# Two-stage attention and a maxout layer on one core: another form of the pooling sums, and the main order without its list of departures

## The chip, the cores and the metric

The kernel runs on one core of a Trainium2 chip. TensorE (PE in the profile) multiplies matrices; a multiplication is a weight load (PEld) and a matmul, and its sums go to PSUM, eight banks of 128 partitions by 512 fp32 numbers. VectorE (DVE), ScalarE (ACT) and GpSimd (POOL) work on tiles; SyncE (SP) and POOL issue transfers. Each engine takes its own instructions in the order in which the program gives them, and waits for others by semaphores. The metric is the time of one execution in microseconds (us) on the device, the median of several; less is better.

## The reference

The input is x of 4 batches by 12,544 tokens by 128 channels, 32 inducing points of 128 channels, and the three weights of a maxout layer with 1,024 hidden units. All is fp32.

```python
def mab(q, kv):
    s = scale * (q @ kv.transpose(0, 2, 1))
    s = s - s.max(-1, keepdims=True)
    a = np.exp(s)
    a /= a.sum(-1, keepdims=True) + 1e-09
    return a @ kv
h = mab(I, x)          # pooling: 32 rows per batch, each a mean of the batch's tokens
y = mab(x, h)          # each token: a mean of its batch's 32 rows of h
g = np.maximum(y @ w1, y @ w2)
out = g @ w_out
```

So each batch must first be pooled over all its tokens to h, and only then can its tokens go through the second attention and the layer.

## The kernel before

**The main part.** Each token's y is a mean of 32 rows of h, weighted by e = exp(scale x h). So the layer is taken on h first: `hwd` is h (w2 - w1) and `m1` belongs to h w1 w_out; a block of 16 chunks of 128 tokens lies in four quarters of 32 partitions each. Per block PE makes e by a *stage* (four matmuls, column mode: four tiles of 32 columns side by side), then *phases* (`phase`, L969 in the profile, row mode: four tiles of 32 rows side by side), whose results are passed through a relu by ACT (L985) or DVE (L988), then *finals* (`final_one`, L792, the full array), 3,136 of them, 128 x 128 each, which multiply the relus by w_out and sum over the hidden units. `dens` (L622) sums e to denominators, `evict_group` (L819) divides and stores through SP.

**The pooling of the next batch** runs beside it, batches 1 to 3. The tokens of a batch are 98 chunks: six units of 16 and a rest of two. Its steps:

- `load_x` (POOL) brings x in seven parts as fp16; a small copy to `pace` holds these loads back until a given sum is there.
- `transpose_x_dma` (L171) has SP transpose x by transfers, 14 half parts; the first unit's scores need the first three of them.
- `pool_scores` (L309, column mode) makes the scores of a unit; ACT makes exp of them, E, and their sums into a column of `es` (L320). `pool_turn` (L346) has SP transpose E to `eT`.
- `pool_accum` (L357, column mode) sums E x over a unit's chunks in one bank of PSUM; DVE adds the bank to `hacc` in SBUF (L382, L385). After the last unit the rest's two chunks are added (L370), with their sums of E in a 129th column.
- `small_rep` (L401) sums the sums of E over the four groups of partitions by an fp32 matmul with `repd`; DVE takes the reciprocal and scales `hacc` (L404, L406). `small_h` (L430) sums h over the groups and transposes it by another fp32 matmul. `small_hwd` (L464) and `small_m1` (L484) follow.

**What sets the order.** The order of each engine's instructions is written when the program is made, by a planner in Python: a class `Clock` (`ck`) adds up what each step is charged, `bank` takes the PSUM bank that comes free first, and a loop chooses the next step for PE. Side steps have due times, counted in finished chunks (`at`), and are ready when the clock says that their inputs are (`ready`). Column steps (scores, accumulations, stages) are taken by `column_work` when PE is in column mode anyway, when two are waiting, or when one is late. A change of the array's mode is charged about 0.1 us. In the loop a list, `DEV`, gives 84 numbered steps at which the choice departs from the rule: 1 puts a phase off, 2 takes it up to 0.2 us earlier, 3 leaves column work out, 4 takes it at once.

The rule itself, and how `DEV` alters it:

```python
now = tp <= ck.pe + early or tp <= tf and tf > ck.pe
if how == 1 and tf < INF:
    now = False
if how == 2 and tp <= ck.pe + 0.2:
    now = True
```

Of the kernel before, what the change touches and what calls it, by code (L numbers as in the profile page):

```python
# [9 lines left out]
F16 = mybir.dt.float16  # L10
F32 = mybir.dt.float32
# [5 lines left out]
INF = 1e9  # L17
# [85 lines left out]
def kernel(  # L103
# [93 lines left out]
    with tc.manual_schedule(engines={ET.PE, ET.DVE, ET.Activation, ET.Pool, ET.SP}):  # L197
# [103 lines left out]

        def pool_scores(b, u):
            if u == 0:
                st[b]["es"] = smp.tile([128, NU + 1], F32, name=f"es_{b}", tag="esu")
                nc.gpsimd.memset(st[b]["es"], 0.0)
            bi, ps = bank([128, 512])
            ck.wait(ck.bank[bi], "p1")
            for g in range(4):
                nc.tensor.matmul(  # L309
                    out=ps[32 * g : 32 * (g + 1), :],  # L310
                    lhsT=inducingT,
                    rhs=xT_tiles[b % 2][:, U * u + 4 * g : U * u + 4 * (g + 1), :],
                    start=True,
                    stop=True,
                    tile_position=(0, 32 * g),
                    skip_group_check=True,
                )
            end = ck.run(0.226, "col")
            eu = etp.tile([128, 512], F16, name=f"eu_{b}_{u}", tag="eu", bufs=NEU)
            nc.scalar.activation(  # L320
                out=eu, in_=ps, func=AF.Exp, scale=scale, accum_out=st[b]["es"][:, u : u + 1]
            )
            ck.bank[bi] = ck.on_act(end, 0.65)
            st[b]["eu", u] = eu, ck.bank[bi]
# [22 lines left out]
            st[b]["eT", u] = eT, ck.pe  # L347

        def pool_accum(b, u):
            bi, ps = bank([128, 512])  # L350
            ck.wait(ck.bank[bi], "p1")
            eT = st[b]["eT", u][0]
            st[b]["sum", u] = True
            last = u == NU - 1
            for j in range(4):
                for g in range(4):
                    nc.tensor.matmul(  # L357
                        out=ps[32 * g : 32 * (g + 1), 0:128],
                        lhsT=eT[:, j, 32 * g : 32 * (g + 1)],
                        rhs=xn_of(b, U * u + 4 * g + j),  # L360
                        start=(j == 0),
                        stop=(j == 3 and not (last and g < REST)),
                        tile_position=(0, 32 * g),
                        skip_group_check=True,
                    )
            if last:
                et = st[b]["et"][0]
                for g in range(REST):
                    for rhs, lo, n in ((xn_of(b, U * NU + g), 0, 128), (ones16[:, 0:1], 128, 1)):
                        nc.tensor.matmul(  # L370
                            out=ps[32 * g : 32 * (g + 1), lo : lo + n],
                            lhsT=et[:, g, :],
                            rhs=rhs,
                            start=False,
                            stop=True,
                            tile_position=(0, 32 * g),
                            skip_group_check=True,
                        )
            end = ck.run(0.26, "col")
            if u == 0:  # L380
                st[b]["hacc"] = smp.tile([128, C], F32, name=f"hacc_{b}", tag="hacc")
                nc.vector.tensor_copy(out=st[b]["hacc"], in_=ps[:, 0:128])  # L382
            else:
                acc = st[b]["hacc"]
                nc.vector.tensor_add(out=acc, in0=ps[:, 0:128], in1=acc)  # L385
            ck.bank[bi] = ck.on_dve(end, 0.2)
            if last:
                es = st[b]["es"]
                nc.vector.tensor_copy(out=es[0 : 32 * REST, NU : NU + 1], in_=ps[0 : 32 * REST, 128:129])
                esr = smp.tile([128, 1], F32, name=f"esr_{b}", tag="esr")  # L390
                nc.vector.reduce_sum(out=esr, in_=es, axis=AX.X)  # L391
                st[b]["esr"] = esr
                ck.bank[bi] = st[b]["esrr"] = ck.on_dve(end, 0.2)
                if b + 1 < B:
                    for i in range(7):
                        load_x(b + 1, i, esr if i == 0 else None)

        def small_rep(b):
            bi, ps = bank([128, 512])
            ck.wait(ck.bank[bi], "p1")  # L400
            nc.tensor.matmul(out=ps[:, 0:1], lhsT=repd, rhs=st[b]["esr"], start=True, stop=True)  # L401
            end = ck.run(0.11)
            rec = smp.tile([128, 1], F32, name=f"rec_{b}", tag="rec")
            nc.vector.reciprocal(out=rec, in_=ps[:, 0:1])  # L404
            acc = st[b]["hacc"]
            nc.vector.tensor_scalar(out=acc, in0=acc, scalar1=rec, scalar2=None, op0=ALU.mult)  # L406
            ck.bank[bi] = st[b]["haccr"] = ck.on_dve(end, 0.4)

        def small_h(b):
            hT4 = smp.tile([C, 4, M], F16, name=f"hT4_{b}", tag="hT4")  # L410
            if b == 0:
# [13 lines left out]
                ready = ck.on_act(st[0]["end"], 0.2)  # L425
                st[b]["hT4"] = hT4.rearrange("c q m -> c (q m)")
                return es, ready
            bi, ps = bank([128, 512])
            ck.wait(ck.bank[bi], "p1")
            nc.tensor.matmul(out=ps[:, 0:128], lhsT=st[b]["hacc"], rhs=repd, start=True, stop=True)  # L430
            end = ck.run(0.25)
            nc.vector.tensor_copy(out=hT4.rearrange("c q m -> c (q m)"), in_=ps[:, 0:128])
            ck.bank[bi] = st[b]["hT4r"] = ck.on_dve(end, 0.2)
            st[b]["hT4"] = hT4.rearrange("c q m -> c (q m)")
# [434 lines left out]
        def want_linear():  # L869
# [9 lines left out]
            return g  # L879

        LINEAR_AHEAD = 18


        DEV = {
            0: 1, 27: 1, 32: 1, 35: 2, 52: 1, 87: 2, 157: 3, 168: 1, 169: 4, 181: 2, 244: 2, 247: 1, 397: 4,
            443: 3, 469: 4, 476: 1, 495: 1, 518: 1, 527: 4, 539: 3, 558: 3, 636: 2, 690: 1, 751: 1, 758: 4,
            764: 3, 765: 1, 773: 1, 778: 1, 835: 1, 858: 1, 866: 1, 867: 1, 869: 1, 972: 1, 992: 4, 1011: 2,
            1013: 3, 1014: 4, 1025: 2, 1029: 1, 1052: 1, 1083: 2, 1113: 1, 1125: 1, 1141: 2, 1179: 1, 1195:
            1, 1215: 4, 1216: 1, 1271: 1, 1296: 2, 1301: 1, 1305: 1, 1324: 1, 1357: 1, 1358: 1, 1387: 4,
            1407: 4, 1428: 1, 1460: 4, 1462: 1, 1488: 4, 1491: 1, 1575: 1, 1579: 1, 1580: 1, 1585: 4, 1601:  # L890
            3, 1625: 2, 1658: 3, 1723: 1, 1736: 3, 1739: 1, 1764: 1, 1777: 1, 1796: 4, 1801: 3, 1812: 1,
            1843: 1, 1966: 3, 1981: 1, 1997: 1, 2021: 1
        }
        LIMIT = -16

        def plan_phase(linear=True):
# [106 lines left out]
        for b in range(1, B):  # L1003
            base = DONE0[b - 1]
            t_first, t_step = (6, 2.2) if b == 1 else (-6, 3.4)
            for u in range(NU):
                if b == 1:
                    s, turn, acc = 25 + 5 * u, 45 + 1.5 * u, 55 + 2 * u
                else:
                    s = turn = 13 + 8.2 * u  # L1010
                    acc = s + 12
                at(base + int(s), pool_scores, b, u)
                at(base + int(turn), pool_turn, b, u)
                at(base + int(acc), pool_accum, b, u)
            s, end = int(s), base + int(acc)
            at(base + s + 2, pool_rest, b)
            at(end, small_rep, b)
            at(end, small_h, b)
            at(end, small_hwd, b)
            at(end, small_m1, b)  # L1020
            for j in range(14):
                at(base + int(t_first + t_step * j), transpose_x_dma, b, j)
# [45 lines left out]
                pending.remove(job)  # L1068
                f(*a)

        def column_work(banks, soon=False):

            if sorted(ck.bank)[banks - 1] > ck.pe + 0.12:
                return False
# [3 lines left out]
                return True  # L1078
            jobs = [job for job in pending if job[0] in COL and ready(*job)]
            late = jobs and (chunks_done[0] >= due[jobs[0]] + 8 or jobs[0][1][1] == NU - 1)  # L1080
            if jobs and (soon or ck.mode == "col" or len(jobs) > 1 or late):
                pending.remove(jobs[0])
                f, a = jobs[0]
                f(*a)
# [14 lines left out]
                "hT4" in st[qu.b] and "hwd" in st[qu.b] for qu in blocks[k0].quarters if qu  # L1099
            )  # L1100


        phase(plan_phase(False))
        weights_3()
        phase(plan_phase(False))
# [1 line left out]
        state["stage"] = 2  # L1107
        weights_1b()
        START = ck.pe
        step = -1  # L1110
        while state["g"] < len(groups) or held:
            step += 1
            how = DEV.get(step, 0)
            side_work()
            if held and ck.mode == "full":
                linear_last(0.0)
            if ck.mode != "full" and how != 3 and column_work(1):
                continue
            if min(ck.bank) <= ck.pe + 0.1 and want_stage(1):
                stage(blocks[state["stage"]])  # L1120
# [7 lines left out]
                fr = sorted(ck.bank)[len(jobs) - 1]  # L1128
                tp = max([fr - 0.095] + [(a.blk.staged if kind == "L" else a.staged) for kind, q, a, u in jobs])
            early = 0.2 if ck.mode == "col" else 0.0  # L1130
            now = tp <= ck.pe + early or tp <= tf and tf > ck.pe
            if how == 1 and tf < INF:
                now = False
            if how == 2 and tp <= ck.pe + 0.2:
                now = True
            if tp < INF and lag() <= 128 + LIMIT and now:
                if how != 3 and column_work(len(jobs) + 1, how == 4):
                    continue
                phase(jobs)
            elif tf < INF:  # L1140
# [8 lines left out]
            else:  # L1149
                raise AssertionError(("stuck", state, ptr, chunks_done, jobs, pending[:3]))  # L1150
        assert not pending and not jobs_at

# [28 lines left out]
```

## Time and profile before

| what | value |
|---|---|
| time, median of 3 runs | 329.54 us (329.04 to 329.61) |
| profiled execution, its own time | 329.54 us |
| its span, first to last instruction | 327.6 us |
| PE busy | 321.6 us, 98% |
| DVE busy | 284.8 us, 87% |
| ACT busy | 281.0 us, 86% |
| finals (L792), steps | 3,136 |
| the add to `hacc` (L385), each of 15 | 0.288 us |

A group of the profile is one line and engine with its output and inputs; `xN` is how many instructions it has, then their busy time and the mean of one, then the idle time of the engine ahead of them and what ended it. The lengths of PE's instructions overlap, since matmuls are pipelined: what a step costs is read from the start of one matmul to the start of the next, not from its length. The chain of waits follows the work that ended last back to the start. In the timeline a row is a run of equal instructions: its start, its length, the engine, the line and the tiles. The transfers are listed by queue (q1 is that of SP's transfers, q0 that of POOL's): packets, megabytes, and the share of 16 engines' time in the stretch asked for; and by issue: how many, and how long from issue to landing.

### The profile page before, as it was taken

The numbers are of one execution on the slowest core, as the hardware profiler recorded it, in microseconds if no ns is written. First come the engines' busy times: TensorE is split into PE (matmuls) and PEld (weight loads), VectorE is DVE, ScalarE is ACT, GpSimd is POOL, SyncE is SP. The second block draws the span as 40 slices with busy tenths as digits, with TensorE's granted clock in tenths as the row PEclk, the third lists the DMA queues.
The fourth block names the chain that finished last, engine by engine and source line by source line (L and its number), as shares of the span: only waits on it lengthen the run. The fifth ranks groups of instructions, "written<-read, shape, count | busy, mean of one in ns | idle before, by whom it ended". The sixth has DMA issues, their size and how long they took to land.

```text
span 327.6 us, 12592 instructions
## 1 busy us (share of the span) xinstructions
PE 321.6 (98%) x5401; PEld 243.8 (74%) x5401; DVE 284.8 (87%) x532; ACT 281.0 (86%) x562; POOL 25.8 (8%) x54
## 2 busy tenths in 40 slices
PE   7999999999999999999999999999999999999996
PEld 3886777777777777777777777777777777778785
DVE  2359998999989999998989989989999989989873
ACT  3679899998789998988988999989969999899961
POOL 7451030000310000000040000000000000000000
PEclk9999999999999999999999999999999999999999
DMA  7999999964299998953579999992422212222233
GB/s 205 207 207 211 288 247 205 236 150 139 57 228 244 228 232 204 197 131 109 121 131 246 217 257 207 182 187 98 132 98 79 101 66 100 98 98 99 83 114 113
DMA packets 70823, 53.65 MB, mean 164 GB/s; under 512 B 52176, under 2 KB 55408, under 8 KB 70768
## 3 DMA queue, kind: packets, MB, share of 16 engines
q1 hardware_dynamic: 64656, 38.63, 47.8%
q0 software_dynamic: 6112, 14.22, 22.2%
q8 instruction: 42, 0.69, 0.9%
q14 instruction: 13, 0.11, 0.1%
HBM read 28.33 MB, written 25.69 MB: 165 GB/s over the span
## 4 chain that ended last, share of the span: by engine, by line
PE 94%; DVE 2%; ACT 1%; DMA 1%; issue 1%; DVEq 0%; ACTq 0%
PE ps L792 60%; PE ps L969 22%; PE ps L582 3%; PE ps L232 2%; PE ps L357 1%; PE ps L309 1%; DMA xf<-in_x_dram 1%; PE ps L248 1%; ACT relu L985 1%; DVE relu L988 1%; PE ps L280 1%; PE ps L622 1%; PE ps L749 1%; PE ps L271 1%; PE ps L640 0%
## 5 line engine op out<-in xcount | busy, mean ns | idle before, releaser
L985 ACT ACTIVATE relu<-ps 128x512 f16<-128x512 f32 x463 | 244.8, 603 | 28.9 <-PE ps L969 20.6
L988 DVE TENSOR_SCALAR relu<-ps 128x512 f16<-128x512 f32 x321 | 205.6, 681 | 18.2 <-PE ps L969 17.3
L792 PE MATMUL ps<-woutp,relu 128*128 128x128 f16 x3136 | 218.1, 220 | 0.1
L792 PEld LDWEIGHTS <-relu 128*128 128x128 f16 x3136 | 177.2, 98 | 40.4 <-issue 30.1
L969 PE MATMUL ps<-e,hwd 32*128 32x512 f16 (+2 forms) x880 | 88.6, 360 | 0.0
L819 DVE TENSOR_TENSOR o<-ps,rp 128x512 f32<-128x512 f32 (+3 forms) x108 | 68.5, 635 | 6.0 <-PE ps L792 3.7
L969 PEld LDWEIGHTS <-hwd 32*128 32x128 f16 x880 | 24.7, 91 | 21.0 <-issue 0.8
L969 PE MATMUL ps<-m,e 32*128 32x128 f16 x381 | 38.7, 217 | 0.0
L969 PEld LDWEIGHTS <-e 32*128 32x128 f16 x381 | 21.4, 92 | 2.6
L165 POOL DMA_DIRECT2D xn<-in_x_dram x31 | 16.9, 555 | 8.2 <-DMA xn<-in_x_dram 4.3
L236 DVE COPY xT<-ps 128x512 f16<-128x512 f16 (+3 forms) x11 | 5.5, 504 | 8.1 <-PE ps L232 8.0
L594 ACT ACTIVATE e<-ps 128x512 f16<-128x512 f32 (+2 forms) x21 | 11.6, 570 | 0.0
L320 ACT ACTIVATE eu<-ps 128x512 f16<-128x512 f32 x18 | 10.8, 616 | 0.0
L582 PE MATMUL ps<-xT,hT 128*32 128x512 f16 (+3 forms) x114 | 10.2, 366 | 0.0
L164 POOL COPY pace<-esr 128x1 f32<-128x1 f32 x2 | 0.4, 184 | 116.2 <-DVE esr L391 116.2
L239 ACT COPY xT<-ps 128x768 f16<-128x768 f16 (+3 forms) x11 | 6.1, 557 | 3.0 <-PE ps L232 2.8
L232 PE MATMUL ps<-identity,xn 128*128 128x128 f16 x98 | 7.7, 223 | 0.2
L232 PEld LDWEIGHTS <-xn 128*128 128x128 f16 x98 | 5.9, 100 | 1.5 <-DVE xn L644 1.0
L582 PEld LDWEIGHTS <-hT 128*32 128x32 f16 x114 | 2.9, 93 | 5.3 <-issue 4.2
L257 ACT ACTIVATE et<-ps 128x448 f16<-128x448 f32 (+4 forms) x11 | 4.5, 413 | 2.6 <-PE ps L248 2.6
L632 DVE RECIPROCAL rp<-ps 128x16 f32<-128x16 f32 (+2 forms) x28 | 6.7, 239 | 0.0
L622 PE MATMUL ps<-ones_q,e 128*128 128x4 f16 x102 | 6.5, 165 | 0.0
(96 smaller groups left out, 117.0 us busy)
## 6 DMA issues: line engine op xcount, KB each, us to landing
out_dram<-o SPq DMA_DIRECT2D x90, 256.0 KB, 2.5
xn<-in_x_dram POOLq DMA_DIRECT2D x24, 448.0 KB, 11.9
out_dram<-o SPq DMA_DIRECT2D x10, 128.0 KB, 3.7
xn<-in_moe_w_dram POOLq DMA_DIRECT2D x4, 256.0 KB, 14.1
xn<-in_x_dram POOLq DMA_DIRECT2D x4, 224.0 KB, 10.2
xT<-xn SPq DMA_TRANSPOSE x42, 3.9
xf<-in_x_dram SPq DMA_DIRECT2D x1, 512.0 KB, 3.8
xf<-in_x_dram SPq DMA_DIRECT2D x1, 384.0 KB, 4.3
```

Source lines behind the costliest of these rows:

```text
L165: nc.gpsimd.dma_start(out=xn_at[b, i][:, 0:n, :], in_=xr[b, :, k0 : k0 + n, :])
L232: nc.tensor.transpose(ps[:, j, :], xn[:, g + j, :], identity16)
L320: nc.scalar.activation(out=eu, in_=ps, func=AF.Exp, scale=scale, accum_out=st[b]["es"][:, u : u + 1])
L582: nc.tensor.matmul(out=ps[32 * q : 32 * (q + 1), 128 * t : 128 * (t + n)], lhsT=hq, rhs=xT[:, c : c + n, :], start=True, stop=True, tile_p ...
L594: nc.scalar.activation(out=blk.e2[:, 0 : 128 * wd], in_=ps[:, 0 : 128 * wd], func=AF.Exp, scale=st[0]["rs"] if blk.b == 0 else scale,)
L622: nc.tensor.matmul(out=ps[:, 4 * t : 4 * t + 4], lhsT=blk.e2[:, 128 * t : 128 * (t + 1)], rhs=ones_q, start=True, stop=True,)
L632: nc.vector.reciprocal(out=blk.rp[:, 0:wd, :].rearrange("p t q -> p (t q)"), in_=ps[:, 0 : 4 * wd])
L792: nc.tensor.matmul(out=g.ps[:, 128 * c : 128 * (c + 1)], lhsT=g.blk.relu[q][:, 128 * (jb * w4 + t) : 128 * (jb * w4 + t + 1)], rhs=woutp[: ...
L819: nc.vector.tensor_mul(osb[:, 0:n, :], g.ps[:, 0 : n * C].rearrange("p (s c) -> p s c", s=n), rp)
L969: nc.tensor.matmul(**seq[i])
L985: nc.scalar.activation(out=dst, in_=src, func=AF.Relu)
L988: nc.vector.tensor_scalar(out=dst, in0=src, scalar1=0.0, scalar2=None, op0=ALU.max)
```

## The change

Two things change together.

First, batches 1 to 3 are pooled in another form. An accumulation now takes two units at a time in one bank, so there are three per batch instead of six, and DVE adds to `hacc` three times instead of six. `hacc` has a 129th column for the sums of E: the reduction of the six sums of ACT goes there ahead of the last accumulation's matmuls, and the rest's sums come with the last add; in the groups without a rest chunk a matmul with a zero tile (`warm`) writes that column. The copy into `es`, the second reduction and POOL's memset of `es` are gone. `small_rep` multiplies `repd` with all 129 columns in fp32, and DVE scales the result to fp16, `h4`; `small_h` transposes `h4` in fp16. The loads of the next batch are held back by the last add instead of the second reduction.

Second, the loop has no list `DEV`: the rule alone chooses.

```diff
-                nc.gpsimd.memset(st[b]["es"], 0.0)
...
         def pool_accum(b, u):
...
+            if u == 1:
+                st[b]["hacc"] = smp.tile([128, C + 1], F32, name=f"hacc_{b}", tag="hacc")
+            acc = st[b]["hacc"]
+            if last:
+                nc.vector.reduce_sum(out=acc[:, C : C + 1], in_=st[b]["es"], axis=AX.X)
+                ck.on_dve(st[b]["eu", u][1], 0.1)
+            for v in (u - 1, u):
+                eT = st[b]["eT", v][0]
+                st[b]["sum", v] = True
+                for j in range(4):
+                    for g in range(4):
+                        nc.tensor.matmul(
+                            out=ps[32 * g : 32 * (g + 1), 0:128],
+                            lhsT=eT[:, j, 32 * g : 32 * (g + 1)],
+                            rhs=xn_of(b, U * v + 4 * g + j),
+                            start=(j == 0 and v < u),
...
             if last:
                 et = st[b]["et"][0]
-                for g in range(REST):
-                    for rhs, lo, n in ((xn_of(b, U * NU + g), 0, 128), (ones16[:, 0:1], 128, 1)):
+                for g in range(4):
+                    pairs = [(warm[:, 0:M], ones16[:, 0:1], 128, 1)]
+                    if g < REST:
+                        pairs = [
+                            (et[:, g, :], xn_of(b, U * NU + g), 0, 128),
+                            (et[:, g, :], ones16[:, 0:1], 128, 1),
+                        ]
...
-            end = ck.run(0.26, "col")
...
+            end = ck.run(0.58 if last else 0.49, "col")
+            n = C + 1 if last else C
+            if u == 1:
+                nc.vector.tensor_copy(out=acc[:, 0:n], in_=ps[:, 0:n])
             else:
-                nc.vector.tensor_add(out=acc, in0=ps[:, 0:128], in1=acc)
-            ck.bank[bi] = ck.on_dve(end, 0.2)
+                nc.vector.tensor_add(out=acc[:, 0:n], in0=ps[:, 0:n], in1=acc[:, 0:n])
+            ck.bank[bi] = ck.on_dve(end, 0.22)
             if last:
-                nc.vector.tensor_copy(out=es[0 : 32 * REST, NU : NU + 1], in_=ps[0 : 32 * REST, 128:129])
-                nc.vector.reduce_sum(out=esr, in_=es, axis=AX.X)
...
+                    load_x(b + 1, i, acc[:, C : C + 1] if i == 0 else None)

         def small_rep(b):
-            nc.tensor.matmul(out=ps[:, 0:1], lhsT=repd, rhs=st[b]["esr"], start=True, stop=True)
-            end = ck.run(0.11)
+            nc.tensor.matmul(out=ps[:, 0 : C + 1], lhsT=repd, rhs=st[b]["hacc"], start=True, stop=True)
+            end = ck.run(0.28)
...
-            nc.vector.tensor_scalar(out=acc, in0=acc, scalar1=rec, scalar2=None, op0=ALU.mult)
+            h4 = smp.tile([128, C], F16, name=f"h4_{b}", tag="h4")
+            nc.vector.tensor_scalar(out=h4, in0=ps[:, 0:C], scalar1=rec, scalar2=None, op0=ALU.mult)
...
         def small_h(b):
-            nc.tensor.matmul(out=ps[:, 0:128], lhsT=st[b]["hacc"], rhs=repd, start=True, stop=True)
-            end = ck.run(0.25)
+            nc.tensor.transpose(ps[:, 0:128], st[b]["h4"], identity16)
+            end = ck.run(0.056)
...
-        DEV = {
-            0: 1, 27: 1, 32: 1, 35: 2, 52: 1, 87: 2, 157: 3, 168: 1, 169: 4, 181: 2, 244: 2, 247: 1, 397: 4,
...
-                at(base + int(acc), pool_accum, b, u)
+                if u % 2:
+                    at(base + int(acc), pool_accum, b, u)
...
-            if ck.mode != "full" and how != 3 and column_work(1):
+            if ck.mode != "full" and column_work(1):
...
-            now = tp <= ck.pe + early or tp <= tf and tf > ck.pe
-            if how == 1 and tf < INF:
-                now = False
-            if how == 2 and tp <= ck.pe + 0.2:
-                now = True
-            if tp < INF and lag() <= 128 + LIMIT and now:
-                if how != 3 and column_work(len(jobs) + 1, how == 4):
+            if tp < INF and lag() <= 128 + LIMIT and (tp <= ck.pe + early or tp <= tf and tf > ck.pe):
+                if column_work(len(jobs) + 1):
```

## The prediction

> **What bounds the kernel now.** I read the page first, then the groups by shape, the timeline around the pooling steps, and the transfers.
>
> The page says that TensorE (PE) is the path: busy 98%, 94% of the chain, at full clock.
>
> ```profile
> span 327.6 us, 12592 instructions
> ...
> PE 321.6 (98%) x5401; PEld 243.8 (74%) x5401; DVE 284.8 (87%) x532; ACT 281.0 (86%) x562; POOL 25.8 (8%) x54
> ...
> PE 94%; DVE 2%; ACT 1%; DMA 1%; issue 1%; DVEq 0%; ACTq 0%
> ```
>
> VectorE (DVE) and ScalarE (ACT) are idle about 40 us each, so only what PE issues, or what PE waits for, moves the end. One cycle of the main part (timeline, PE alone; start, length):
>
> ```profile
> 157.52 0.96 PE L792 MATMUL ps<-woutp,relu 128*128 128x128 f16 x14
> 158.41 0.39 PE L969 MATMUL ps<-e,hwd 32*128 32x512 f16 x4
> 158.74 0.95 PE L792 MATMUL ps<-woutp,relu 128*128 128x128 f16 x14
> ```
>
> From 157.52 to 158.74 is 1.22 us: 14 finals (L792) at 0.056, a row phase (L969) of 0.22 (the step between two 512-column matmuls of L464 is 0.216), and two changes of tile mode at 0.1 each. A visit in row mode thus costs 0.43, of which 0.33 lies between its first matmul and the next final. Nothing else fits in: PE waits nowhere in this cycle.
>
> The first of the three small steps of the pooling, batch 1, PE and DVE (two answers of the timeline):
>
> ```profile
> 85.78 0.41 PE L357 MATMUL ps<-xn,eT 128*32 128x128 f16 x16
> ...
> 87.27 0.23 PE L792 MATMUL ps<-woutp,relu 128*128 128x128 f16 x1
> 87.57 0.35 PE L401 MATMUL ps<-esr,repd 128*128 128x1 f32 x2
> 87.79 0.22 PE L792 MATMUL ps<-woutp,relu 128*128 128x128 f16 x1
> ```
>
> ```profile
> 86.83 0.28 DVE L385 TENSOR_TENSOR hacc<-ps,hacc 128x128 f32<-128x128 f32 x1
> 87.03 0.13 DVE L389 COPY es<-ps 64x1 f32<-64x1 f32 x1
> 87.27 0.16 DVE L391 TENSOR_REDUCE esr<-es 128x1 f32<-128x7 f32 x1
> ```
>
> A final is followed by the next matmul after 0.056; here `small_rep` starts 0.30 behind it, since it waits for the sum that ended at 87.43. In batches 2 and 3 these are 0.47 (163.77 to 164.24) and 0.36.
>
> **The change part by part**, on PE's path, for three batches.
>
> 1. *h.* The fp32 matmul (L430) is two passes: 241.59 to the next final at 241.87 is 0.28. The fp16 transpose has the form of L484, one 128x128 step of 0.06. Three times 0.22: **-0.66**. Its price lies between the plain step and the old one, so the ends are -0.66 and 0.
>
> 2. *small_rep with 129 columns.* L401 takes 0.22 to the next final (87.57 to 87.79); with 128 columns L430 takes 0.28. **+0.19**, ends 0 and +0.4 (twice that step).
>
> 3. *The wait in front of small_rep.* Beyond 0.056 it is 0.24 + 0.41 + 0.30 = 0.95 today. The copy and the second reduction (86.83 + 0.28 to 87.43, 0.32) leave the chain, because the reduction of ACT's sums is issued ahead of the matmuls and the rest arrives as column 129 of the add. But the step also comes closer behind the accumulation (3 finals in batch 1 instead of 11), and the add itself can stand behind a relu of 0.68 on DVE, as at 85.04 to 86.92. The planner charges the copy and the reduction 0.2 (line 393 and its neighbours) where the trace has 0.32, and so issues the step too early today; the add it charges 0.22 against 0.29. Hence I keep a wait of 0.1 a batch: **-0.65**, ends -0.95 (no wait) and +1.1 (a relu of 0.68 more in each batch, less the 0.32).
>
> 4. *Mode changes.* In the order of the built kernels PE enters row, column and full mode 482 times before and 484 after: accumulations share visits, but without the 84 departures stagings and scores stand alone more often (column visits 34 to 37). 2 x 0.1 = **+0.2**. The matmuls of pooling are the same 288; the six extra ones into column 129 run beside others in column mode: **+0.05**, ends 0 and 6 x 0.056.
>
> 5. *DVE and POOL.* Nine adds or copies of 0.288 and three copies fall away, about 3 us of 284.8; three memsets of POOL too. DVE is off the path: 0. What hides it is PE's stream of finals; where DVE is late for a relu, the gain would show as a shorter wait, which is in point 7.
>
> 6. *What the later accumulation pushes back.* In the order the last accumulation of batch 1 stands behind final 638 instead of 580, and the first scores of batch 2 ahead of final 912 instead of 1014. The accumulation releases the next batch's loads (`pace`), the loads fill the DMA engines, and the x transposes on SP's queue move only behind them:
>
> ```profile
> 87.49 0.18 POOL L164 COPY pace<-esr 128x1 f32<-128x1 f32 x1 [43.56 <-DVE esr L391]
> ```
>
> ```profile
> q0 software_dynamic: 202, 0.66, 82.9%
> q1 hardware_dynamic: 202, 0.31, 24.0%
> ...
> xT<-xn SPq DMA_TRANSPOSE x1, 9.4
> ```
>
> ```profile
> q1 hardware_dynamic: 2312, 0.90, 87.2%
> ...
> xT<-xn SPq DMA_TRANSPOSE x3, 3.9
> ```
>
> The second is 104 to 108 us (loads on q0 still running; the transpose lands after 9.4 us), the third 112 to 116 (loads done; 3.9). PE's rows up to the accumulation: 58 finals more (3.25), 3 visits in row mode more (1.3), four denominators (0.1), one unit less accumulated (-0.22): it starts 4.4 us later than today's 85.78; the shorter DVE chain and the longer accumulation about cancel, so pace is at 91.8. Today the seventh load lands 22.3 us behind pace (109.8), in batch 3 23.2: 114.1 to 115.0 then. The first scores need the third transpose, which lands 4.2, 5.4 and 4.0 us after the last load in the three batches: 118.1 to 120.4. The scores, 127.20 today (landing 115.2, 12 us to spare), come earlier: 102 finals fewer (-5.7), 8 visits in row mode fewer (-3.4), one staging with its mode changes fewer (-0.4), points 1 and 3 (-0.4): near 117.2. So PE, which takes its instructions in order, would stand 0.9 to 3.2 us in front of them. Counted instead from the first transpose's issue (it keeps its place, about 104.4, and the third lands 11.4 to 11.9 us behind it in all batches) it lands at 115.8 to 116.3: no wait. I take **+1.2**, nearer to the count from the loads because q1 hardly moves until they end, with ends 0 and +3.2. Behind the waiting matmul all finals and phases queue, so ACT and DVE run dry too; nothing of the sort can be negative, since in the old order nothing waits there. The accumulations of two units wait for both transposes of their exponents; the closest, units 2 and 3 of batch 2, stand at 150 us by the order and the transposes landed at 144.8: 0, a wait on PE if that cover goes. Batch 3's scores keep 5 us to spare (199.5 against a landing of 191.5 plus 1.6 of later pace), batch 1's loads don't move. SP itself: the stores behind the transposes are issued later, but batch 3 had its loads and transposes overlap 8 us and PE shows no wait there.
>
> A sentence by itself: the Trainium skill, "DMA: Bandwidth & Descriptors", section "Queues, rings and completion order", says that each DMA engine takes turns between the queues a packet at a time; if the transposes got such a share they would land in time, and the sum would be 1.2 us lower, 329.2.
>
> 7. *The order without its departures.* PE's other waits after the ramp (phases with more than 0.33 to the next final, at 32.7, 34.0, 73.7, 85.3, 86.8, 94.2 us and a few column visits) come to about 1.0 us. In the new order the shortest distances are tighter: a phase reuses a bank under 1.2 us behind its last writer 87 times instead of 78, an accumulation's bank 0.60 us behind instead of 0.83, a denominators' bank 0.63 instead of 1.34. At 85.3 and 86.8 such distances cost 0.19 and 0.12. Three or four more of these: **+0.4**, ends -1.0 (all today's waits gone) and +1.5.
>
> Sum: -0.66 + 0.19 - 0.65 + 0.2 + 0.05 + 1.2 + 0.4 = +0.73. The profiled execution took 329.54, the median of the runs (span 327.6, 1.9 outside it): **330.3 us**, slower by 0.22%.
>
> **The rivals.**
> A. *The transposes are in time* (point 6 is 0), and the rest holds: 329.1, not slower. For it: the count from the first transpose's issue, and three batches with the same 11.4 to 11.9. Against it: their packets move only once q0 is empty. It decides if the third transpose lands before 117.2.
> B. *They come last* by the loads' count, 3.2 us: 332.3. For it: batch 2 had the longest lag, 5.4. Against it: more transposes will be waiting when the loads end.
> C. *The departures were worth more*, point 7 at its upper end with 1.2 at the scores: 331.4. For it: bank distances. Against it: DVE has 3 us less to do.
> D. *The small steps gain nothing*, as another wait takes the place of the old one (point 3 at 0, +0.65; the transpose waiting for the scaled h as long as L401 did for its sum, +0.95): 331.9. For it: the transpose stands 8 to 16 finals behind `small_rep`, where L430 stood 21 to 23 behind L401. Against it: between them DVE needs only 0.16 and 0.29 us (the rows of L404 and L406), and L430 showed no wait.
>
> **How the numbers follow.** My case 0.45, A 0.27, B 0.10, C 0.12, D 0.06. My case alone spans 329.4 to 331.2; about 0.2% (0.66 us) is what a measurement can tell from no change. Of my case 0.55 is slower and 0.45 same; of A 0.5 faster, 0.45 same; B, C, D are slower. Faster 0.14, same 0.33, slower 0.53. Range 328.7 (A with the wait in front of `small_rep` all gone) to 332.1.
>
> **What would show it.** A matmul of `pool_scores` in batch 2, near 117 us, with PE idle ahead of it by a DMA of xT, 0.5 to 2 us, and POOL's pace copy near 92 us: point 6. A transpose of h one plain step long, a gap ahead of `small_rep` of 0.1 to 0.2: points 1 and 3. PE's matmuls as busy as before elsewhere: points 4 and 7. I am wrong if PE never stops at the scores (then A), or if many phases wait for banks (C).

## The result and the profile after

The changed kernel takes **330.99 us** (median of 6 runs, 330.16 to 331.23), the kernel before, run beside it, 329.74 (6 runs, 329.04 to 330.07). The ratio is 1.0034, with an interval of 1.0019 to 1.005: slower by about 1.1 us. The profiled execution took 331.03 us.

The page of the changed kernel, its head and the chain:

```profile
span 329.0 us, 12585 instructions
...
PE 322.2 (98%) x5404; PEld 243.0 (74%) x5404; DVE 283.2 (86%) x521; ACT 281.5 (86%) x561; POOL 25.4 (8%) x51
...
PE 96%; DMA 1%; DVE 1%; issue 1%; ACT 0%; SPq 0%; ACTq 0%
PE ps L801 59%; PE ps L966 22%; PE ps L591 2%; PE ps L232 2%; PE ps L308 1%; PE ps L364 1%; DMA xT<-xn 1%; PE ps L657 1%; PE ps L248 1%; PE ps L280 1%; PE ps L631 1%; PE ps L649 1%; PE ps L758 1%; PE ps L271 1%; PE ps L473 0%
```

DVE has 11 instructions less and is 1.6 us less busy, and yet the span is 1.4 us longer. The new thing is in the group of the scores, which had no such wait before, and in the chain, where a transfer of xT now has a place. The group's row before and after (busy, mean ns of one, then idle time ahead of it and what ended it):

```profile
L309 PE MATMUL ps<-xT,inducingT 128*32 128x512 f16 x72 | 6.2, 382 | 0.0
...
L308 PE MATMUL ps<-xT,inducingT 128*32 128x512 f16 x72 | 6.6, 383 | 1.2 <-DMA xT<-xn 1.2
```

The place is the first scores of batch 2, in the timeline of PE (start, length):

```profile
116.85 0.40 PE L966 MATMUL ps<-e,hwd 32*128 32x512 f16 x4
117.17 0.40 PE L591 MATMUL ps<-xT,hT 128*32 128x512 f16 x4
117.40 0.39 PE L308 MATMUL ps<-xT,inducingT 128*32 128x512 f16 x3
118.97 0.38 PE L308 MATMUL ps<-xT,inducingT 128*32 128x512 f16 x1 [1.19 <-DMA xT<-xn]
119.28 0.25 PE L631 MATMUL ps<-ones_q,e 128*128 128x4 f16 x4
```

The visit in column mode starts at 117.17 with a stage; three of the four scores matmuls go through, and the fourth, which reads the third transposed part, waits until 118.97. From 117.17 to the next step at 119.28 is 2.11 us; eight such matmuls and the next step's start take 0.54 where nothing is waited for (the first experiment shows it). So PE stood **1.57 us**. The profile's own 1.19 is less, since it counts idle time only from the modelled end of the last matmul.

Why the part was late, in the timelines of POOL and SP (DMA issues; the length is that of the issuing):

```profile
91.74 0.18 POOL L164 COPY pace<-hacc 128x1 f32<-128x1 f32 x1 [47.66 <-DVE hacc L397]
91.98 3.74 POOL L165 DMA_DIRECT2D xn<-in_x_dram  x7
```

```profile
104.36 1.23 SPq L171 DMA_TRANSPOSE xT<-xn  x1
105.68 1.98 SPq L853 DMA_DIRECT2D out_dram<-o  x1
107.72 5.95 SPq L171 DMA_TRANSPOSE xT<-xn  x1
113.75 0.53 SPq L853 DMA_DIRECT2D out_dram<-o  x1
114.39 1.22 SPq L171 DMA_TRANSPOSE xT<-xn  x1
```

The pace copy came at 91.74 instead of 87.49. The seventh load landed at 113.94 instead of 109.80, the third transpose at 118.93 instead of 115.19. SP shows its queue held up while the loads run: the second transpose took 5.95 us to issue, and the third was issued only at 114.39, behind the landing of the last load.

The small steps of batch 1, PE and DVE (two answers of the timeline):

```profile
91.54 0.34 PE L801 MATMUL ps<-woutp,relu 128*128 128x128 f16 x3
91.82 0.46 PE L409 MATMUL ps<-hacc,repd 128*128 128x129 f32 x2
92.12 1.00 PE L801 MATMUL ps<-woutp,relu 128*128 128x128 f16 x15
...
93.06 0.22 PE L439 MATMUL ps<-identity,h 128*128 128x128 f16 x1
93.12 0.55 PE L801 MATMUL ps<-woutp,relu 128*128 128x128 f16 x7
```

```profile
90.53 0.15 DVE L357 TENSOR_REDUCE hacc<-es 128x1 f32<-128x6 f32 x1
91.38 0.29 DVE L397 TENSOR_TENSOR hacc<-ps,hacc 128x129 f32<-128x129 f32 x1 [0.70 <-PE ps L383]
```

`small_h` (L439) is one plain step, 93.06 to 93.12. `small_rep` (L409) takes 0.30, 91.82 to 92.12, and starts 0.15 behind the end of the add (91.38 + 0.29). From the last final ahead of each step to the next final behind it, less the plain step of 0.056, the two steps take 2.45 us in three batches before and 1.68 after. So the new steps do what they should; what was won there, and more, was lost at 117.4.

Two profiled executions can't be compared by their ends alone: before the first final of the main part lies a start-up whose length varies by about half a microsecond between executions (the changed kernel's was 0.37 later there than the kernel's before, other runs were 0.4 to 0.5 earlier or later). Below, traces are compared at the same final, counted from the first one. So counted, the changed kernel is ahead by 0.8 to 0.9 at finals 600 and 900, behind by 0.55 at final 1050 and by 1.6 at final 1350, and by about 1.0 from final 3000 to the end.

### The profile page after: what moved, and what is told of

It is laid out like the page before. It is cut to its first block, busy times and chain, and to the rows that moved or that the text cites. A ratio compares the mean times of both kernels' runs of the same rounds, so it can differ in the third digit from the quotient of the medians.

```text
span 329.0 us, 12585 instructions
## 1 busy us (share of the span) xinstructions
PE 322.2 (98%) x5404; PEld 243.0 (74%) x5404; DVE 283.2 (86%) x521; ACT 281.5 (86%) x561; POOL 25.4 (8%) x51
## 2 busy tenths in 40 slices
DMA packets 70823, 53.65 MB, mean 163 GB/s; under 512 B 52176, under 2 KB 55408, under 8 KB 70768
## 4 chain that ended last, share of the span: by engine, by line
PE 96%; DMA 1%; DVE 1%; issue 1%; ACT 0%; SPq 0%; ACTq 0%
PE ps L801 59%; PE ps L966 22%; PE ps L591 2%; PE ps L232 2%; PE ps L308 1%; PE ps L364 1%; DMA xT<-xn 1%; PE ps L657 1%; PE ps L248 1%; PE ps L280 1%; PE ps L631 1%; PE ps L649 1%; PE ps L758 1%; PE ps L271 1%; PE ps L473 0%
## 5 line engine op out<-in xcount | busy, mean ns | idle before, releaser
L308 PE MATMUL ps<-xT,inducingT 128*32 128x512 f16 x72 | 6.6, 383 | 1.2 <-DMA xT<-xn 1.2
L631 PEld LDWEIGHTS <-e 128*128 128x128 f16 x102 | 5.4, 97 | 2.1 <-issue 1.9
```

What stands on the lines that cost most here:

```text
L308: nc.tensor.matmul(out=ps[32 * g : 32 * (g + 1), :], lhsT=inducingT, rhs=xT_tiles[b % 2][:, U * u + 4 * g : U * u + 4 * (g + 1), :], start ...
L631: nc.tensor.matmul(out=ps[:, 4 * t : 4 * t + 4], lhsT=blk.e2[:, 128 * t : 128 * (t + 1)], rhs=ones_q, start=True, stop=True,)
```

## The experiments

**1. The stop alone.** In the changed kernel the loads of batch 2 are released by the transpose of the last E of batch 1 instead of the last add. The order of PE, DVE, ACT and SP is the same.

```diff
             st[b]["eT", u] = eT, ck.pe
+            if b == 1 and u == NU - 1:
+                for i in range(7):
+                    load_x(b + 1, i, eT[:, 0, 0:1] if i == 0 else None)
...
-            if last and b + 1 < B:
+            if last and 1 < b < B - 1:
```

> The changed kernel, with one thing moved: batch 2's loads are released by the landing of the last transposed exponents of batch 1 instead of by the last add to hacc, some 5 us earlier; PE, DVE, ACT and SP have the same instructions in the same order. Theory (the loads hold the x transposes back, and PE stops 1.2 us, with the latency 1.5 us, in front of the first scores of batch 2): the third transpose lands by 115 us, the gap at the scores is gone, and the kernel takes 1.2 to 1.5 us less than the changed one, 329.5 to 329.8. Rival (the stop costs nothing at the end, since later waits would come anyway; the order without departures is the cause): the gap goes, the time stays within 0.4 us of 331.0.

Measured: 328.83 us against 329.36 of the kernel before, ratio 0.9986 (0.9976 to 0.9995). Timeline of PE at the same place:

```profile
116.35 0.40 PE L594 MATMUL ps<-xT,hT 128*32 128x512 f16 x4
116.57 0.39 PE L308 MATMUL ps<-xT,inducingT 128*32 128x512 f16 x4
116.89 0.25 PE L634 MATMUL ps<-ones_q,e 128*128 128x4 f16 x4
```

The pace copy came at 84.07, the third transpose landed at 112.37, and the four scores run without a gap: 0.54 from 116.35 to 116.89. Against the changed kernel the trace is 0.83 ahead (start-up) up to final 900 and 2.38 from final 1050 to the last. The stop is worth 1.55 us, a little more than the 1.2 to 1.5 that were expected, and PE never makes it up. Without it the new pooling under the plain rule is a little faster than the kernel before.

**2. The departures alone.** The kernel before with an empty list.

```diff
-        DEV = {
-            0: 1, 27: 1, 32: 1, 35: 2, 52: 1, 87: 2, 157: 3, 168: 1, 169: 4, 181: 2, 244: 2, 247: 1, 397: 4,
...
+        DEV = {}
```

> The kernel before with an empty list of departures: the rule alone, the old pooling. By the order its first scores of batch 2 stand ahead of final 1014 as before, so nothing waits for the transposes there; PE changes its mode 485 times instead of 482. Theory: 0.3 us for the modes and some 0.4 for waits at banks, 330.2 to 330.6. Rival (the departures are the whole cause): as slow as the changed kernel, 331.0. Second rival (they are worth nothing): 329.7.

Measured: 330.53 against 329.36, 1.0033 (1.0021 to 1.0044), +1.1 us; expected was +0.7. So the list was worth a microsecond to the old pooling. By the time alone this is the same as the changed kernel, and a reader of times could take the departures for the whole story. The trace speaks against it, and so does experiment 1, where the rule alone with the new pooling is not slower than before: here the scores of batch 2 stand at final 1014 and PE waits for no transfer. The loss, 0.91 us from the first final on, is spread out: 485 mode changes against 482 (0.3 by the planner's 0.1 each), and 0.36 more in the row visits. The wait ahead of `small_rep` is 0.17 longer in batch 3 but 0.16 shorter in batch 2, so it adds nothing; the remaining 0.25 isn't placed. The changed kernel loses its time at one place. With the empty list the old pooling keeps the scores at 1014, so it takes the new pooling to bring them forward; the new pooling with the old list was not run.

**3. The small steps alone.** The kernel before, its order and its single accumulations kept, with the 129th column, the 129-column `small_rep` and the fp16 transpose.

```diff
-            nc.tensor.matmul(out=ps[:, 0:1], lhsT=repd, rhs=st[b]["esr"], start=True, stop=True)
+            nc.tensor.matmul(out=ps[:, 0 : C + 1], lhsT=repd, rhs=st[b]["hacc"], start=True, stop=True)
...
-            nc.tensor.matmul(out=ps[:, 0:128], lhsT=st[b]["hacc"], rhs=repd, start=True, stop=True)
+            nc.tensor.transpose(ps[:, 0:128], st[b]["h4"], identity16)
```

> The kernel before, its order of every engine kept, with the new small steps alone: the sums of E as a 129th column, small_rep with 129 columns, h by an fp16 transpose; the accumulations stay one unit each. Theory: 3 x 0.22 less for h, 3 x 0.08 more for small_rep, and 0.3 to 0.9 less wait in front of it: 0.7 to 1.3 us less than before, 328.4 to 329.0. Rival (PE's gain is given back at the next wait for a relu or a bank): within 0.3 us of before.

Measured: 329.08 against 329.36, 0.999 (0.9981 to 0.9998); 0.28 us less by the medians, as the rival had it, 0.6 by the trace. The theory was too hopeful, though its terms came: -0.22 a batch for h, +0.08 for `small_rep`, and in the three batches together 0.55 less wait ahead of it: -0.96 in all. Of this 0.36 was lost again. The timeline of PE behind the transpose of batch 1:

```profile
89.54 0.22 PE L435 MATMUL ps<-identity,h 128*128 128x128 f16 x1
89.59 1.06 PE L797 MATMUL ps<-woutp,relu 128*128 128x128 f16 x16
90.58 0.56 PE L974 MATMUL ps<-e,hwd 32*128 32x256 f16 x6
91.08 0.23 PE L797 MATMUL ps<-woutp,relu 128*128 128x128 f16 x1
```

The transpose saves 0.22, but the next phase, 90.58 to 91.08, takes 0.50 instead of 0.33: it waits 0.17, and nothing is left of batch 1's gain. In batch 2 a phase waits 0.19 in the same way, and 0.19 of the gain is left; batch 3 keeps 0.38. The profile doesn't name what this phase waits for; a bank whose reader on DVE or ACT comes no earlier than before would do it, but that is argued and not shown.

**4. h by fp32 again.** The changed kernel, same order, with `h4` in fp32 and a matmul by an fp32 identity.

```diff
-            h4 = smp.tile([128, C], F16, name=f"h4_{b}", tag="h4")
+            h4 = smp.tile([128, C], F32, name=f"h4_{b}", tag="h4")
...
-            nc.tensor.transpose(ps[:, 0:128], st[b]["h4"], identity16)
+            nc.tensor.matmul(out=ps[:, 0:128], lhsT=st[b]["h4"], rhs=identity32, start=True, stop=True)
```

> The changed kernel with one step put back to fp32: h is transposed by an fp32 matmul with the identity, two passes, in the same place of the same order. Theory: 0.22 us more per batch, 0.66 in all, 331.4 to 331.8. Rival (the small step hides behind other waits): within 0.3 us of the changed kernel's 331.0.

Measured: 331.11 against 329.36, 1.006 (1.0045 to 1.0074). That is 0.0026 above the changed kernel's ratio, 0.86 us, though the two intervals overlap. In the trace the three steps cost 0.25, 0.15 and 0.26 more, and the stop at the scores is 0.17 shorter, as PE arrives there later: 0.49 in all from the first final on. The price of the step is as predicted; of the 0.25 that it cost ahead of the stop, 0.17 came back there, since the stop ends when the transfer lands.

**5. The loads later still.** The changed kernel with the pace copy of batch 2 made nine times.

```diff
-            nc.gpsimd.tensor_copy(out=pace, in_=after)
+            for _ in range(9 if b == 2 else 1):
+                nc.gpsimd.tensor_copy(out=pace, in_=after)
```

> The changed kernel with the loads of batch 2 held back longer: POOL makes the pace copy nine times instead of once (0.18 us each, about 1.5 to 1.9 us more); PE, DVE, ACT and SP as in the changed kernel. Theory: the third transpose lands later by as much, and the stop in front of the scores and the whole kernel grow by 1.5 to 1.9 us, to 332.5 to 332.9. Rival (the stop has another cause, or a longer one is made up for later): 331.0.

Measured: 331.71 against 329.30, 1.0075 (1.0055 to 1.0094), 0.0041 above the changed kernel. Timeline of PE:

```profile
116.73 0.40 PE L592 MATMUL ps<-xT,hT 128*32 128x512 f16 x4
116.96 0.38 PE L309 MATMUL ps<-xT,inducingT 128*32 128x512 f16 x1
118.59 0.39 PE L309 MATMUL ps<-xT,inducingT 128*32 128x512 f16 x2 [1.25 <-DMA xT<-xn]
119.50 0.38 PE L309 MATMUL ps<-xT,inducingT 128*32 128x512 f16 x1 [0.52 <-DMA xT<-xn]
119.81 0.25 PE L632 MATMUL ps<-ones_q,e 128*128 128x4 f16 x4
```

Now the second matmul waits already. The loads were issued 2.0 us later, the third transpose landed 0.96 later (119.46; start-up taken off), and the visit from 116.73 to 119.81 is 0.97 longer. The direction is that of the theory and the stop follows the landing, but the size expected was too large: a delay of the loads isn't passed on whole. The last load landed 1.65 later, and the third transpose, issued here at 113.54 while loads were still running, landed 4.3 us behind the last load instead of 5.0.

**6. The same delay in the old order.** The kernel before with the same edit, nine copies.

> The kernel before with the same nine pace copies ahead of batch 2's loads, all else the same. There the scores stand 12 us behind the landing of their transposes. Theory: no change, within 0.3 us of before. Rival (later loads cost by themselves, by the DMA engines or the stores): 1 us or more slower than before.

Measured: 329.28 against 329.30, 0.9997 (0.9987 to 1.0006). The third transpose landed at 116.13 and the scores stand far behind it. Nothing is wrong with late loads as such; it needs the early scores too.

**7. The scores later.** The changed kernel, with the planner told that the transposes of batch 2 need 14 us instead of 8.

```diff
-                return d.get(("T", (U * a[1] + U - 1) // (P1 // 2)), INF) + 8.0 <= now
+                return d.get(("T", (U * a[1] + U - 1) // (P1 // 2)), INF) + (14.0 if a[0] == 2 else 8.0) <= now
```

> The changed kernel, with the planner charging 14 us instead of 8 from the issue of a transpose to its use by the scores of batch 2; the order changes from there on, and the first scores stand ahead of final 979 instead of 912 as a visit of their own. Theory: no stop in front of them, 1.3 to 1.6 us less than the changed kernel, less 0.2 to 0.4 for another column visit or two: 329.6 to 330.0. Rival: the new order brings other waits, 330.5 or more.

Measured: 328.95 against 329.30, 0.9981 (0.997 to 0.9992). The order puts the scores at final 979, at 123.27 us; the third transpose lands at 118.66, as in the changed kernel (start-up taken off), and the group of the scores shows no idle time. From the first final on the trace gains 1.74 on the changed kernel, more than the 1.0 to 1.4 that were expected: 1.55 to 1.57 is the stop, and in the new order `small_rep` of batch 2 waits 0.10 instead of 0.28. Either end of the wait can be moved; this one leaves the transfers alone.

**8. Eleven new departures.** The changed kernel with the loop code of the kernel before and a list that a search made for the new pooling, by the planner's own clock; `small_rep` is charged 0.3.

```diff
+        DEV = {19: 2, 58: 1, 206: 2, 485: 1, 486: 1, 580: 1, 596: 1, 1117: 1, 1165: 2, 1208: 1, 1729: 1}
```

> The changed kernel with departures of its own: eleven steps at which the order departs from the rule (step 19, 206 and 1165 take a phase earlier, eight others put one off), and 0.3 us charged for small_rep instead of 0.28. By the order PE changes its mode 480 times instead of 484, the last accumulation of batch 1 stands behind final 610 instead of 638, and the first scores of batch 2 ahead of final 982 instead of 912. Theory: no stop at the scores (1.6 us less), 0.4 us less for modes, and fewer waits at banks by 0.1 to 0.5: 2.1 to 2.5 us less than the changed kernel, 328.5 to 328.9 beside a kernel before of 329.5, so at or below the kernel with early loads. Rival (any departure from the rule helps only the order that it was made for, as a matter of chance): 329.5 or more.

Measured: **327.52** against 329.53, 0.9939 (0.9925 to 0.9953): 2.0 us faster than the kernel before, more than expected. Its page:

```profile
span 325.2 us, 12584 instructions
...
PE 319.3 (98%) x5404; PEld 242.6 (75%) x5404; DVE 282.0 (87%) x519; ACT 281.8 (87%) x563; POOL 25.4 (8%) x51
```

It changes mode 480 times, the last accumulation of batch 1 stands behind final 610 instead of 638, the scores ahead of final 982 (the third transpose landed at 115.06), and what the row visits take beyond their plain 0.33 adds up to 0.8 us, where the changed kernel's adds up to 1.3. From the first final on the trace is 2.87 ahead of the changed kernel. The stop (1.55), the row visits (0.5), four mode changes less (0.4 by the planner's price) and a wait ahead of `small_rep` of 0.31 instead of 0.59 in three batches make 2.7 of it; each was read from the trace, and none was tried alone.

**9. Both.** The same with the loads of experiment 1.

> The same, and batch 2's loads released by the landing of batch 1's last transposed exponents. PE's order is the same as with the eleven departures alone. Theory: the scores stand behind the landing of their transposes either way, so the loads make no difference: within 0.3 us of the eleven departures alone. Rival (the transposes still hold PE back somewhere): 0.5 to 1.5 us less.

Measured: 327.54 against 329.53, 0.9939 (0.9926 to 0.9953), no difference from 8. Where the scores aren't early, earlier loads are worth nothing.

## Why the prediction was right, and where its sizes were off

Predicted were 330.3 us, slower, and a stop at the scores of batch 2 as the largest term. By its own points:

- **1, h: right.** -0.66 as predicted: 0.055 a step against 0.28, and experiment 4 buys it back.
- **2, `small_rep`: near.** 0.296, 0.297 and 0.326 against 0.215: +0.27 instead of +0.19.
- **3, the wait ahead of it: mis-sized.** Kept was 0.10, 0.28 and 0.21, in all 0.59 of the 0.95, not 0.1 a batch: -0.36 instead of -0.65. The mechanism that the prediction feared is the one seen, in the timeline of DVE in batch 2:

```profile
165.88 1.28 DVE L985 TENSOR_SCALAR relu<-ps 128x512 f16<-128x512 f32 x2
167.08 0.15 DVE L357 TENSOR_REDUCE hacc<-es 128x1 f32<-128x6 f32 x1
167.33 0.29 DVE L397 TENSOR_TENSOR hacc<-ps,hacc 128x129 f32<-128x129 f32 x1
```

  PE's accumulation was over at 166.39, but DVE had two relus running until 167.16, and the reduction, meant to be out of the way by then, stood between them and the add. The add ended at 167.62 and `small_rep` started at 167.77. Taking two instructions off the chain moved the wait to what stands before them on DVE.
- **4, mode changes: the count, 484, is that of the order.** The price of +0.25 wasn't isolated.
- **5, DVE and POOL: nothing,** as said. DVE is 1.6 us less busy, not 3; one relu more, 0.68, fell to it (322 against 321). No run tried its lower load alone.
- **6, the stop: right in place and chain, a bit small.** The pace copy was predicted at 91.8 and came at 91.74, the last load at 114.1 to 115.0 (113.94), the scores at 117.2 (117.40), the third transpose by the loads' count at 118.1 to 120.4 (118.93). The measured times hold 0.37 of a later start-up, which all of them share. The stop was put at 1.2, inside 0 to 3.2, and is 1.55. That the loads and not the first transpose's issue set the landing was the choice that decided the sign, and it held: the third transpose landed 14.6 us behind the first one's issue, not 11.4 to 11.9. The 1.2 itself was picked between two counts, 0 and 0.9 to 3.2, not added up. In batch 3 the scores had 8.0 us to spare; the prediction said 5, though its own numbers (199.5 against 191.5 plus 1.6) make 6.4.
- **7, the order without departures: too dear.** What the 220 row visits take beyond 0.33 adds up to 1.30 us, 1.16 before: 0.14 more, where three or four longer waits at banks were put. With points 1 to 3 at their measured sizes and 4 as predicted, -0.50, experiment 1's -0.46 leaves +0.04 where +0.4 was put. The departures were worth 1.1 us, but to the old pooling (experiment 2); the new pooling under the rule alone has no such loss to show.

The sum with these sizes: -0.50 + 0.04 + 1.55 = +1.1, the ratio's 1.1; as the +0.04 is what experiment 1 leaves over, this says that the stop is the difference between experiment 1 and the changed kernel, and is no check of point 7. Points 3 and 6 were each 0.3 too small in cost, point 7 was nearly 0.4 too large, so the total came out 0.4 low: that the misses partly cancel is luck.

**The rivals.** A, transposes in time, fell, but its price, 0.4 below the kernel before, is nearly what experiments 1 and 7 measure once the stop is taken away (0.5 and 0.6 below, by the ratios). B, the full 3.2 us, fell: the lag behind the last load was 5.0 us, but the last load was earlier than the count had it. C, many more waits for banks, fell by the row visits. Of D's 1.6 us 0.3 came: `small_rep` kept 0.59 of its wait, 0.29 more than was put, and the transpose of h never waited.

**The rule on the queues.** The prediction cited the Trainium skill, "DMA: Bandwidth & Descriptors", section "Queues, rings and completion order": an engine takes turns between the queues a packet at a time. The counts agree with the rule, and the conclusion drawn from it, that such a share would bring the transposes in time, did not hold (A's 329.1 is also the sum without the stop, not the 329.2 given there). The transfers of the changed kernel at 104 to 108 us, loads still running, and at 112 to 116, with 35 packets of the loads left and the last load landed at 113.94 (packets, MB, share of 16 engines' time):

```profile
q0 software_dynamic: 215, 0.67, 83.2%
q1 hardware_dynamic: 214, 0.31, 24.1%
...
xT<-xn SPq DMA_TRANSPOSE x2, 9.4
```

```profile
DMA packets 2477, 0.87 MB, mean 217 GB/s; under 512 B 2201, under 2 KB 2457, under 8 KB 2477
...
q1 hardware_dynamic: 2442, 0.80, 106.6%
q0 software_dynamic: 35, 0.07, 8.9%
```

215 packets against 214: turns one for one. But a load's packet holds 3.1 KB, and nine in ten of those in the second stretch, where the transposes run, hold less than 512 B. By an estimate from the profile's page of the changed kernel (52,176 packets under 512 B, shared out by elements over the 42 transposes of x and 18 of E) one transpose of x has about 1,000 packets. At 54 packets a microsecond, some of them the stores', it hardly moves; with the loads ending the queue gets about 600 (2,442 in 4 us). A fair turn was a share of packets, not of bytes.

## What to carry to other kernels

When a step is moved, follow what it releases to the next engine that needs it, and set both times against each other: here a pace copy 4.2 us later and scores 100 finals earlier met at one matmul, and PE, which works in order, lost 1.55 us for good. A list of exceptions to a planner's rule belongs to the order it was found for: dropping it cost the old form 1.1 us, and a new one of eleven entries gave the new form 1.3 (traces) to 1.5 us (ratios) more than the rule without the stop (experiments 8 and 1). Before giving up a change that is slower by a little, look for the one wait that makes it so: with that wait moved the same pooling is about half a microsecond faster than the kernel before.

## What the runs showed that was not expected

- While POOL's loads are queued, SP's queue gets as many packets as theirs, whatever their size: in two stretches of 2 us each, 108 to 112 us of the changed kernel, 108 against 109 and 95 against 92; from 114 to 116, loads done, it moved 1,590. The counts part before the last load lands: in experiment 5, whose last load landed at 115.16, 106 stand against 270 from 112 to 114.
- Loads that start 2.0 us later make the third transpose only 0.96 later (experiment 5). What shortens the way was not tried.
- A saving of 0.22 us on PE was given back at a later phase by 0.17 and 0.19 in two of three batches (experiment 3), while a stop of 1.55 us on PE was not made up in the 2,200 finals behind it (experiment 1).
- The fp32 matmul of 129 columns takes 0.185 from its first pass to its second and 0.11 from there to the next final, 0.296 in all, in two of three batches, and 0.326 in the third; the one-column form took 0.215. A hundred and twenty-eight more columns cost 0.08 to 0.11.
